# The first 60 microseconds of a fused retention and SiLU kernel: weight slice first, filler multiplies, transposes issued in parts

## The chip, the cores and the metric

The kernel runs on one core of a Trainium2 chip. Its engines are TensorE (PE in the profile; its weight loads are PEld), VectorE (DVE), ScalarE (ACT), GpSimd (POOL) and SyncE (SP), which only issues DMAs here. Each engine works through its own queue in order; they meet through semaphores. The metric is the device time of one execution in microseconds; lower is better.

## The reference

A recurrent retention layer is followed by a feed-forward block. q, k and v are 4 batches x 8 heads x 768 steps x 64 in float32; the two weights arrive as float64 (512 x 2048 and 2048 x 512).

```python
for t in range(S):
    state = gamma[None, :, None, None] * state + np.einsum('bhd,bhe->bhde', k[:, :, t], v[:, :, t])
    y[:, :, t] = scale * np.einsum('bhd,bhde->bhe', q[:, :, t], state)
...
x = np.ascontiguousarray(attn_out.transpose(0, 2, 1, 3)).reshape(B * S, H * D)
h = x @ w_in
g = h * (1.0 / (1.0 + np.exp(-h)))
return (g @ w_out).astype(np.float32)
```

## The kernel before

**Units.** The sequence is cut into 6 chunks of 128 steps. A unit is one chunk of one batch with all 8 heads; units are numbered chunk by chunk, so units 0 to 3 are chunk 0 of the four batches. For each unit the kernel

- loads k, q and v, 256 KB each, by one DMA each on SP's queue (`load`, L158);
- `T(n)` (`stage_t`): turns k and q, four 128x128 transposes each on TensorE (kp, qp), which ScalarE copies to SBUF (kt, qt);
- `K(n)` and `Q(n)`: scale k in place and the turned q by powers of gamma on VectorE; `KA(n)` does the former by eight instructions on ScalarE;
- `SC(n)`: 32 products of k with v (`stage_s`, the sums for the state; they read the scaled k) and 32 products of k with q (`stage_a`, the scores; they read kt and the scaled qt);
- `A(n)`, called three times (`steps_a`): the scores times a decay mask (am, L470), then the state in the middle of the chunk (mid), then the state behind it;
- `YA(n)` and `YB(n)` (`stage_y`): am with v, then q with the states, in two parts; between the parts stands a fence, a memset on POOL that waits for the first part and releases the second;
- `X(n)`, called four times (`steps_y`, `split_x`): copy y from PSUM (ys, L542), and split it into three float32r parts, xh on ScalarE (L557), xl (L560) and the third (L563) on VectorE.

**Products with w_in.** w_in is worked through in 16 column slices of 128. A slice is loaded by three DMAs (512 KB in all, `load_w`, two staging buffers) and converted from float64 words and split into three float32r parts in eleven steps, one for each `W(i)` (`early_slice`): the first, the eighth and the tenth are on ScalarE (L196, L120, L126), the other eight on VectorE (L199, L202, L206, L209, L212, L217, L123, L128). `P(n)` multiplies one slice with the four units of one chunk: twelve products of 128x128 by 128x512, eight into ha and four into hb. `CL(n)`, three times, closes it: a copy on ScalarE, a subtraction on VectorE, SiLU on ScalarE; `put_g` sends the result to DRAM. When all 96 results are made, they are read back, split and multiplied with w_out, which is prepared in the same way.

**The order.** TensorE's instructions are issued in program order throughout. For the first part of the kernel, up to `early_order.close()`, those of the other four queues are too: the calls `T(0), K(0)` and so on, one line after another, are the order of every queue. Behind that point the order of VectorE, ScalarE and SP is left to the planner of the framework, with a few instructions tied behind others. Up to that point the order holds units 0 to 7, the slices 0, 1 and 2 and the products P(0), P(1), P(2) with chunk 0 and P(16), which is the first one with chunk 1.

**PSUM.** kp, ha and hb share three banks in turn (`turn`); qp has a bank of its own, the scores and sums have two, y has two.

**The places that the change touches.** The loads at the top put k, q and v of units 0 to 5 on SP's queue in order, with slice 0 behind unit 0 and slice 1 behind unit 3. The identity that the transposes multiply with is made by POOL at 1.0 to 1.3 us. `next_chunk` rescales the powers of gamma for the next chunk by four instructions on ScalarE. `nc.scalar.activation(out=token, ...)` has no use but to load the table of SiLU early.

Of the kernel before, what the change touches and what calls it, by code (L numbers as in the profile page):

```python
# [13 lines left out]
FP32 = mybir.dt.float32  # L14
# [19 lines left out]
def kernel(  # L34
# [131 lines left out]
    def load_w(i):  # L166
        if i >= 2 * NF:
            return
        if wide:
            t = stage.tile([128, 2 * DM], U32, tag="wf", name=f"wf_{i}")  # L170
            w_in, w_out, n = moe_w_in.bitcast(U32), moe_w_out.bitcast(U32), 256
        else:
            t = stage.tile([128, DM], FP32, tag="wf", name=f"wf_{i}")
            w_in, w_out, n = moe_w_in, moe_w_out, 128
        if i < NF:
            to = t.rearrange("p (i o f) -> o p i f", o=2, f=n)
            src = w_in[:, ts(i, n)].rearrange("(i o p) f -> o p i f", o=2, p=128)
            nc.sync.dma_start(out=to[0], in_=src[0])
            for j in range(2):
                nc.sync.dma_start(out=to[1, ts(j, D)], in_=src[1, ts(1 - j, D)])  # L180
        else:
            nc.sync.dma_start(out=t, in_=w_out[ts(i - NF, 128), :])
        staged[i] = t
# [103 lines left out]
    def begin_w():  # L287
# [10 lines left out]
    early_order.enter_context(tc.manual_schedule(engines={  # L298
        mybir.EngineType.SP, mybir.EngineType.DVE, mybir.EngineType.Activation,
        mybir.EngineType.Pool}))  # L300
    for n in range(EARLY - 2):
        for name in "kqv":
            load(name, n)
        if n in (0, 3):
            load_w(n // 3)


    ident = const.tile([128, 128], FP32, tag="ident", name="ident")
# [54 lines left out]
    def banks(tag, name, n=2):  # L363
        return ps_u.tile([128, n, 512], FP32, tag=tag, name=name)
# [3 lines left out]
    def turn(name):  # L368
        turns[0] += 1
        return ps_h.tile([128, 512], FP32, tag=f"h{turns[0] % 3}", name=name)  # L370
# [55 lines left out]
        nc.scalar.copy(out=to[n].bitcast(U16).rearrange("p a (t w) -> p w a t", w=2),  # L426
                       in_=turned.pop((name, n)).rearrange("p (w a) t -> p w a t", w=2))

    def stage_t(n):

        for name, to, bufs, src, tp in (
                ("kt", kt, 2, kqv["k"][n], turn(f"kp_{n}")),
                ("qt", qt, 3, kqv["q"].pop(n), banks("q", f"qp_{n}", 1)[:, 0])):
            tp = tp.rearrange("p (a t) -> p a t", a=HP)
            for a in range(HP):
                nc.tensor.transpose(tp[:, a, :], src[:, 2 * a : 2 * a + 2, :], ident)  # L436
            to[n] = one.tile([128, HP, C], FP32, tag=name, name=f"{name}_{n}", bufs=bufs)
            evac[:] = [nc.scalar.copy(out=to[n], in_=tp).ins]

    def score_tile(n):  # L440
        u = banks("s", f"sc_{n}")
# [90 lines left out]
    def steps_y(n, yp):  # L532
        c, b = units[n]
        if b == 0:
            p, tag = (wpool, "wq") if c == LATE else (xpool, "xt")
            xt[c] = p.tile([128, 3, KIN, NT], FP32R, tag=tag, name=f"xt_{c}")
        raw = None
        if c < LATE:
            if n == 0:
                raws.append(wpool.tile([128, LATE * B, KIN, C], FP32, tag="wq", name="ys"))  # L540
            raw = raws[0][:, n]
            nc.scalar.copy(out=raw.rearrange("p a (o t) -> p o a t", o=2), in_=yp)  # L542
        elif c == LATE:
            raw = hpool.tile([128, KIN, C], FP32, tag="hs", name=f"ys_{n}")
            nc.scalar.copy(out=raw.rearrange("p a (o t) -> p o a t", o=2), in_=yp)
            nc.sync.dma_start(out=y_dram[b], in_=raw)
        yield from split_x(c, b, yp, raw)
# [179 lines left out]

    sa, ys, asteps, ysteps = {}, {}, {}, {}

    def T(n):  # L730
        stage_t(n)

    def SC(n):
        sa[n] = sc, sums = score_tile(n)
        stage_s(n, sums)
        stage_a(n, sc)
        asteps[n] = steps_a(n, sc, sums)

    def A(n):
        next(asteps[n], None)  # L740
# [10 lines left out]
    def X(n):  # L751
        next(ysteps[n], None)
# [12 lines left out]

    K, Q = scale_k, scale_q

    T(0), K(0)
    nc.scalar.activation(out=token, in_=lgc[:1, :1], func=AF.Silu)
    SC(0), A(0), Q(0), A(0), A(0)  # L770
    W(0), W(0), W(0), W(0), W(0)
    YA(0), YB(0), X(0)
    T(1), K(1)
    W(0)
    load_w(2)
    W(0)
    X(0), X(0)
    SC(1), A(1)
    W(0)
    A(1)  # L780
    Q(1), A(1)
    T(2), K(2)
    W(0), X(0)
    W(0), W(0)
    YA(1), SC(2)
    A(2)
    YB(1), X(1)
    A(2), Q(2), A(2)
    X(1)
    T(3), K(3)  # L790
    X(1), X(1)
    YA(2), YB(2), X(2)
    SC(3), A(3), A(3), Q(3), A(3)
    X(2), W(1), W(1)
    X(2), X(2)
    YA(3), YB(3), X(3), X(3)
    W(1), W(1)
    T(4)
    X(3), X(3)
    K(4)  # L800
    W(1), W(1)
    loads(EARLY - 2), loads(EARLY - 1)
    closing = {}

# [7 lines left out]
    def KA(n):  # L812
        t = kqv["k"][n]
        for h in range(H):
            nc.scalar.activation(out=t[:, h, :], in_=t[:, h, :], func=AF.Copy,
                                 scale=gk[:, units[n][0], h : h + 1])

    P(0)
    next_chunk()
    SC(4)  # L820
    CL(0), CL(0), CL(0)
    put_g(0)
    W(1)
    T(5)
    A(4), A(4), Q(4), K(5), A(4)
    W(1), W(1)
    YA(4), SC(5), YB(4)
    loads(EARLY)
    load_w(3)
    W(2), W(1)  # L830
    A(5)
    W(1), W(2), W(2)
    X(4)
    T(6)
    P(1)
    A(5), Q(5), A(5)
    KA(6)
    W(2), W(2), W(2)
    load("k", EARLY + 1), load("q", EARLY + 1)
    load_w(4)  # L840
    W(2)
    CL(1), CL(1)
# [184 lines left out]
```

## Time and profile before

| | us |
|---|---|
| median of 5 runs | 621.65 |
| lowest and highest | 621.46, 623.22 |
| the profiled execution | 621.65 |
| its span | 619.9 |
| TensorE busy | 604.3 (97%) |
| VectorE busy | 422.8 (68%) |
| ScalarE busy | 312.8 (50%) |
| first transpose of unit 0 | 4.18 |
| first product P(0) starts | 28.20 |

The profile is of one execution. Its times count from the start of the span; the execution took 1.75 us more than the span. In a timeline row stand the start, the duration, the engine, the line of the program, the operation, what is written and read, shapes, and how many such instructions follow each other; in brackets the idle time of the engine before it and what ended that. The slices of the page cut the span into 40 equal parts of 15.5 us; a digit is the busy share in tenths. In rows of groups of instructions three durations (least, median, most, in ns) are followed by the start of the first and of the last one.

### The profile page before, as it was taken

How to read it: one execution, taken by the hardware profiler on the slowest of the kernel's cores; microseconds unless marked ns; L12 is line 12 of the kernel's file. 1: busy time of each engine (PE TensorE's matmuls, PEld its weight loads, DVE VectorE, ACT ScalarE, POOL GpSimd, SP SyncE). 2: the span in 40 equal slices, each digit the busy share in tenths (PEclk: the TensorE clock that was granted, in tenths of full speed). 3: DMA queues.
4: the chain of work that ended last, by engine and by line, in shares of the span. 5: the costliest groups of instructions: out<-in, count | busy, mean ns of one | idle time of the engine just before them, and what ended most of it. 6: DMA issues, size and time to landing. Idle time of an engine off the chain costs nothing.

```text
span 619.9 us, 13494 instructions
## 1 busy us (share of the span) xinstructions
PE 604.3 (97%) x5384; PEld 498.0 (80%) x5384; DVE 422.8 (68%) x731; ACT 312.8 (50%) x595; POOL 22.0 (4%) x79
## 2 busy tenths in 40 slices
PE   6898999999999999999999999999999999999997
PEld 5777887888888888788788888888888888888886
DVE  4999889889789876767599783644635454554631
ACT  6678896676654666765587741312221221412311
POOL 3000000000001111110000000000000000000000
PEclk9999999999999999999999999999999999999999
DMA  9999896564667999989767542432523433442301
GB/s 193 218 216 217 221 250 195 167 191 166 221 162 220 247 252 212 264 230 277 271 224 262 194 154 68 156 116 83 186 72 120 153 102 102 138 134 85 120 1 68
DMA packets 137998, 107.31 MB, mean 173 GB/s; under 512 B 94800, under 2 KB 103248, under 8 KB 137936
## 3 DMA queue, kind: packets, MB, share of 16 engines
q1 hardware_dynamic: 135056, 101.21, 57.6%
q10 hardware_dynamic: 2880, 5.24, 2.3%
q8 instruction: 42, 0.69, 0.5%
q14 instruction: 20, 0.16, 0.1%
HBM read 66.06 MB, written 36.70 MB: 166 GB/s over the span
## 4 chain that ended last, share of the span: by engine, by line
PE 82%; ACT 1%; DMA 1%; SPq 0%; issue 0%; DVE 0%; DVEq 0%; POOLq 0%
PE ha L650 24%; PE o L967 21%; PE oa L967 14%; PE hb L650 12%; PE ob L967 7%; PE y L501 2%; PE sc L462 1%; PE sc L452 1%; DMA qw<-qp 1%; PE o L975 0%; SPq L676 0%; PE oa L975 0%; ACT qt L426 0%; PE qp L436 0%; PE kp L436 0%; ACT kt L426 0%
## 5 line engine op out<-in xcount | busy, mean ns | idle before, releaser
L650 PE MATMUL ha<-xt,wi 128*128 128x512 f32 x768 | 193.6, 394 | 1.1 <-ACT xt L557 0.7
L650 PEld LDWEIGHTS ha<-xt,wi 128*128 128x128 f32 x768 | 141.9, 188 | 33.2 <-ACT wi L126 1.2
L967 PE MATMUL o<-wo,gs 128*128 128x512 f32 x564 | 143.2, 389 | 0.0
L717 DVE TENSOR_TENSOR gs<-gr,gs 128x512 fp32r<-128x512 f32 x96 | 62.1, 685 | 90.3 <-ACT gs L715 90.3
L967 PEld LDWEIGHTS o<-wo,gs 128*128 128x128 f32 x564 | 105.9, 188 | 21.9
L715 ACT ACTIVATE gs<-gr 128x512 fp32r<-128x512 f32 x96 | 53.6, 621 | 134.2 <-issue 131.8
L967 PE MATMUL oa<-wo,gs 128*128 128x512 f32 x376 | 115.8, 389 | 0.0
L650 PE MATMUL hb<-xt,wi 128*128 128x512 f32 x384 | 103.1, 390 | 0.8 <-DVE g L665 0.7
L665 DVE TENSOR_TENSOR g<-g,hb 128x512 f32<-128x512 f32 x96 | 65.6, 683 | 44.5 <-ACT g L660 25.9
L650 PEld LDWEIGHTS hb<-xt,wi 128*128 128x128 f32 x384 | 71.8, 188 | 16.9 <-DVE g L665 1.1
L670 ACT ACTIVATE g<-g 128x512 f32<-128x512 f32 x96 | 60.3, 628 | 46.3 <-DVE g L665 46.2
L967 PEld LDWEIGHTS oa<-wo,gs 128*128 128x128 f32 x376 | 70.6, 188 | 14.7
L967 PE MATMUL ob<-wo,gs 128*128 128x512 f32 x188 | 73.7, 392 | 0.0
L660 ACT ACTIVATE g<-ha 128x512 f32<-128x512 f32 x96 | 57.0, 594 | 31.6 <-PE ha L650 13.2
L718 DVE SCALAR_TENSOR_TENSOR gs<-gs 128x512 fp32r<-128x512 f32 x96 | 62.0, 683 | 0.0
L967 PEld LDWEIGHTS ob<-wo,gs 128*128 128x128 f32 x188 | 35.3, 188 | 8.7 <-DVE o L985 1.6
L196 ACT ACTIVATE ca<-wf 128x512 f32<-128x512 f32 x32 | 21.3, 667 | 7.4 <-DVE cw L217 6.2
L212 DVE SCALAR_TENSOR_TENSOR ca<-wf,ca 128x512 f32<-128x512 uint32 x32 | 22.7, 709 | 0.5
L984 ACT ACTIVATE o<-o 128x512 f32<-128x512 f32 x10 | 6.0, 600 | 33.4 <-PE o L967 33.0
L206 DVE SCALAR_TENSOR_TENSOR cs<-ca,cs 128x512 uint32<-128x512 uint32 x32 | 22.1, 690 | 0.9
L501 PE MATMUL y<-qt,mid 64*64 64x64 f32 x384 | 20.3, 224 | 1.5 <-POOL token L377 1.5
L470 DVE TENSOR_TENSOR am<-sc,decay 128x512 f32<-128x512 f32 x24 | 16.5, 686 | 6.1 <-PE sc L462 6.0
(93 smaller groups left out, 562.0 us busy)
## 6 DMA issues: line engine op xcount, KB each, us to landing
gd<-g SPq DMA_DIRECT2D x96, 256.0 KB, 3.2
gr<-gd SPq DMA_DIRECT2D x96, 256.0 KB, 2.7
wf<-in_moe_w_out_dram SPq DMA_DIRECT2D x16, 512.0 KB, 4.4
out_dram<-o ACTq DMA_DIRECT2D x20, 256.0 KB, 2.1
wf<-in_moe_w_in_dram SPq DMA_DIRECT2D x16, 256.0 KB, 4.2
wf<-in_moe_w_in_dram SPq DMA_DIRECT2D x32, 128.0 KB, 4.2
kf<-in_k_dram SPq DMA_DIRECT2D x16, 256.0 KB, 5.2
qf<-in_q_dram SPq DMA_DIRECT2D x16, 256.0 KB, 4.4
```

The source lines that it names most:

```text
L196: nc.scalar.activation(out=a.bitcast(FP32), in_=hi.bitcast(FP32), func=AF.Abs, scale=65536.0)
L206: nc.vector.scalar_tensor_tensor(out=s, in0=a, scalar=3, in1=s, op0=ALU.logical_shift_left, op1=ALU.bitwise_or)
L212: nc.vector.scalar_tensor_tensor(out=p.bitcast(FP32), in0=lo, scalar=2.0 ** -52, in1=p.bitcast(FP32), op0=ALU.mult, op1=ALU.mult)
L501: i = nc.tensor.matmul(yp[ts(e, D), o, a, :], lhsT=lhsT, rhs=rhs, start=(e, o) not in started, stop=True, skip_group_check=True).ins
L650: nc.tensor.matmul(hb if i == 2 else ha, lhsT=w_sb[f][:, i, ts(kk, 128)], rhs=xt[c][:, i, kk, :], start=kk == 0 and i != 1, stop=kk == KIN ...
L660: copied[:] = [nc.scalar.activation(out=hs, in_=ha, func=AF.Copy, scale=ONE_E).ins]
L665: taken_out[:] = [nc.vector.tensor_tensor(out=hs, in0=hs, in1=hb, op=ALU.subtract).ins]
L670: nc.scalar.activation(out=hs, in_=hs, func=AF.Silu)
L715: nc.scalar.activation(out=t[:, 0, :], in_=g, func=AF.Copy, scale=HALF)
L717: nc.vector.tensor_tensor(out=t[:, 1, :], in0=g, in1=high, op=ALU.subtract)
L718: nc.vector.scalar_tensor_tensor(out=t[:, 2, :], in0=t[:, 1, :].bitcast(FP32), scalar=-1.0 / EPS, in1=high, op0=ALU.mult, op1=ALU.add)
L967: nc.tensor.matmul(o, lhsT=g, rhs=wo[f][:, i, :], start=f == 0 and i != 1, stop=f == NF - 1 and i != 0)
```

## The change

Seven things are changed, all in the ordered part:

- slice 0 of w_in is loaded ahead of k, q and v of unit 0; slice 1 stays behind unit 3;
- `keep_busy` is new: it multiplies the identity with itself n times into a bank that nobody reads. 17 such multiplies stand ahead of everything on TensorE, 3 ahead of Y(1), 3 and 2 around the first part of Y(3);
- five conversion steps of slice 0 come ahead of T(0), and the table of SiLU is loaded ahead of T(0) too;
- `stage_t` can turn k and q separately, and the transposes of k and of q stand apart: of unit 1 ahead of YA(0) and behind it, of unit 2 behind YA(1) and behind YB(1), of unit 3 ahead of YA(2) and behind it, of unit 4 ahead of P(0) and behind it;
- for units 0 to 3 the copy ys is left out: xh and xl read y from PSUM. Units 4 to 7 keep the copy;
- `next_chunk` is written ahead of P(0);
- between P(0) and P(1) the steps of slices 1 and 2 are ordered anew, P(1) comes ahead of T(6), and the loads of k and q of unit 9 come ahead of slice 3.

```diff
--- before.py
+++ after.py
@@ -298,11 +298,12 @@
     early_order.enter_context(tc.manual_schedule(engines={
         mybir.EngineType.SP, mybir.EngineType.DVE, mybir.EngineType.Activation,
         mybir.EngineType.Pool}))
+    load_w(0)
     for n in range(EARLY - 2):
         for name in "kqv":
             load(name, n)
-        if n in (0, 3):
-            load_w(n // 3)
+        if n == 3:
+            load_w(1)
 
 
     ident = const.tile([128, 128], FP32, tag="ident", name="ident")
@@ -426,16 +427,24 @@
         nc.scalar.copy(out=to[n].bitcast(U16).rearrange("p a (t w) -> p w a t", w=2),
                        in_=turned.pop((name, n)).rearrange("p (w a) t -> p w a t", w=2))
 
-    def stage_t(n):
-
-        for name, to, bufs, src, tp in (
-                ("kt", kt, 2, kqv["k"][n], turn(f"kp_{n}")),
-                ("qt", qt, 3, kqv["q"].pop(n), banks("q", f"qp_{n}", 1)[:, 0])):
+    def stage_t(n, names="kq"):
+
+        for name in names:
+            if name == "k":
+                to, bufs, src, tp = kt, 2, kqv["k"][n], turn(f"kp_{n}")
+            else:
+                to, bufs, src, tp = qt, 3, kqv["q"].pop(n), banks("q", f"qp_{n}", 1)[:, 0]
             tp = tp.rearrange("p (a t) -> p a t", a=HP)
             for a in range(HP):
                 nc.tensor.transpose(tp[:, a, :], src[:, 2 * a : 2 * a + 2, :], ident)
-            to[n] = one.tile([128, HP, C], FP32, tag=name, name=f"{name}_{n}", bufs=bufs)
+            to[n] = one.tile([128, HP, C], FP32, tag=f"{name}t", name=f"{name}t_{n}", bufs=bufs)
             evac[:] = [nc.scalar.copy(out=to[n], in_=tp).ins]
+
+    def keep_busy(n, t=None):
+        t = turn(f"none_{turns[0]}") if t is None else t
+        for _ in range(n):
+            nc.tensor.matmul(t[:, :128], lhsT=ident, rhs=ident, start=True, stop=True)
+        return t
 
     def score_tile(n):
         u = banks("s", f"sc_{n}")
@@ -535,8 +544,8 @@
             p, tag = (wpool, "wq") if c == LATE else (xpool, "xt")
             xt[c] = p.tile([128, 3, KIN, NT], FP32R, tag=tag, name=f"xt_{c}")
         raw = None
-        if c < LATE:
-            if n == 0:
+        if B <= n < LATE * B:
+            if n == B:
                 raws.append(wpool.tile([128, LATE * B, KIN, C], FP32, tag="wq", name="ys"))
             raw = raws[0][:, n]
             nc.scalar.copy(out=raw.rearrange("p a (o t) -> p o a t", o=2), in_=yp)
@@ -727,8 +736,8 @@
 
     sa, ys, asteps, ysteps = {}, {}, {}, {}
 
-    def T(n):
-        stage_t(n)
+    def T(n, names="kq"):
+        stage_t(n, names)
 
     def SC(n):
         sa[n] = sc, sums = score_tile(n)
@@ -765,40 +774,27 @@
 
     K, Q = scale_k, scale_q
 
+    keep_busy(17)
+    W(0, 5)
+    nc.scalar.activation(out=token, in_=lgc[:1, :1], func=AF.Silu)
     T(0), K(0)
-    nc.scalar.activation(out=token, in_=lgc[:1, :1], func=AF.Silu)
-    SC(0), A(0), Q(0), A(0), A(0)
-    W(0), W(0), W(0), W(0), W(0)
-    YA(0), YB(0), X(0)
-    T(1), K(1)
-    W(0)
+    W(0, 3)
     load_w(2)
-    W(0)
+    SC(0), A(0), W(0), A(0), Q(0), A(0)
+    T(1, "k"), K(1), W(0)
+    YA(0), T(1, "q"), YB(0), W(0)
     X(0), X(0)
-    SC(1), A(1)
-    W(0)
-    A(1)
-    Q(1), A(1)
-    T(2), K(2)
-    W(0), X(0)
-    W(0), W(0)
-    YA(1), SC(2)
-    A(2)
-    YB(1), X(1)
-    A(2), Q(2), A(2)
-    X(1)
-    T(3), K(3)
-    X(1), X(1)
-    YA(2), YB(2), X(2)
-    SC(3), A(3), A(3), Q(3), A(3)
-    X(2), W(1), W(1)
-    X(2), X(2)
-    YA(3), YB(3), X(3), X(3)
-    W(1), W(1)
-    T(4)
-    X(3), X(3)
-    K(4)
-    W(1), W(1)
+    SC(1), X(0), A(1), A(1), Q(1), X(0), A(1)
+    keep_busy(3)
+    YA(1), T(2, "k"), K(2), YB(1), X(1), X(1)
+    T(2, "q"), X(1), X(1)
+    SC(2), A(2), T(3, "k"), A(2), Q(2), K(3), A(2)
+    YA(2), T(3, "q"), YB(2), X(2), X(2)
+    SC(3), X(2), A(3), A(3), Q(3), A(3), X(2)
+    none = keep_busy(3)
+    YA(3), keep_busy(2, none), YB(3), X(3), X(3), W(1), W(1), X(3), X(3)
+    T(4, "k"), K(4)
+    W(1, 3)
     loads(EARLY - 2), loads(EARLY - 1)
     closing = {}
 
@@ -815,28 +811,31 @@
             nc.scalar.activation(out=t[:, h, :], in_=t[:, h, :], func=AF.Copy,
                                  scale=gk[:, units[n][0], h : h + 1])
 
+    next_chunk()
     P(0)
-    next_chunk()
+    CL(0), T(4, "q")
     SC(4)
-    CL(0), CL(0), CL(0)
+    CL(0), CL(0)
     put_g(0)
-    W(1)
+    W(1, 3)
+    A(4)
     T(5)
-    A(4), A(4), Q(4), K(5), A(4)
+    A(4), Q(4), K(5), A(4)
     W(1), W(1)
     YA(4), SC(5), YB(4)
+    W(1)
     loads(EARLY)
+    load("k", EARLY + 1), load("q", EARLY + 1)
     load_w(3)
-    W(2), W(1)
+    W(2)
     A(5)
-    W(1), W(2), W(2)
+    W(2), W(2)
     X(4)
+    P(1)
     T(6)
-    P(1)
     A(5), Q(5), A(5)
     KA(6)
     W(2), W(2), W(2)
-    load("k", EARLY + 1), load("q", EARLY + 1)
     load_w(4)
     W(2)
     CL(1), CL(1)
```

## The prediction

> **What bounds the kernel now.** I read the page's busy shares and slices first, then the waits, the timelines of TensorE and VectorE up to 64 us, and the landing times of the loads.
>
> ```profile
> PE 604.3 (97%) x5384; PEld 498.0 (80%) x5384; DVE 422.8 (68%) x731; ACT 312.8 (50%) x595; POOL 22.0 (4%) x79
> ...
> PE   6898999999999999999999999999999999999997
> ...
> DVE  4999889889789876767599783644635454554631
> ```
>
> TensorE is full from about 64 us to the end (its visible waits after that add up to little more than a microsecond, most of it one of 0.7 at 98), so only the start can be shortened, and a delay that is still there at 64 us reaches the end. In the first four slices VectorE is about as full as TensorE. Its timeline gives the pace: the mask product (am) of each of the first four units.
>
> ```profile
> 5.37 0.69 DVE L398 TENSOR_TENSOR kqv<-kqv,gk 128x512 f32<-128x512 f32 x1 [5.37 <-PE kp L436]
> 8.54 0.69 DVE L470 TENSOR_TENSOR am<-sc,decay 128x512 f32<-128x512 f32 x1 [2.48 <-PE sc L462]
> ...
> 15.70 0.69 DVE L470 TENSOR_TENSOR am<-sc,decay 128x512 f32<-128x512 f32 x1
> ...
> 19.58 0.68 DVE L470 TENSOR_TENSOR am<-sc,decay 128x512 f32<-128x512 f32 x1
> ...
> 23.70 0.69 DVE L470 TENSOR_TENSOR am<-sc,decay 128x512 f32<-128x512 f32 x1 [0.65 <-PE sc L462]
> ```
>
> VectorE idles 5.4 us before its first instruction and 2.5 before the second; from 12.9 to 23.0 it has no gap. Units 1, 2 and 3 follow one another in 3.9 and 4.1 us. The first product, P(0), starts at 28.20. TensorE runs slowly at first:
>
> ```profile
> L436 PE MATMUL kp<-ident,kqv x8: 421/421/472, 4.2 to 12.4; 128*128 128x128 f32 x8
> ...
> L436 PE MATMUL kp<-ident,kqv x4: 272/272/332, 26.8 to 27.2; 128*128 128x128 f32 x4
> ```
>
> The same transposes take 421 ns until 12 us and 272 ns at 27; from issue to issue it is 0.22 and 0.11 us. The switch lies near 17.5, where unit 1's score part of y is short already (0.75 us against 1.14 at 9.3). A third stretch matters, 36 to 42 us:
>
> ```profile
> 36.54 0.66 PE L436 MATMUL kp<-ident,kqv 128*128 128x128 f32 x4
> ...
> 37.39 2.09 PE L650 MATMUL ha<-xt,wi 128*128 128x512 f32 x8
> ...
> 38.25 2.02 ACT L815 ACTIVATE kqv<-kqv,gk 128x64 f32<-128x64 f32 x8
> ...
> 39.32 1.08 PE L650 MATMUL hb<-xt,wi 128*128 128x512 f32 x4
> ...
> 40.18 0.58 ACT L660 ACTIVATE g<-ha 128x512 f32<-128x512 f32 x1
> ...
> 41.08 0.65 PE L452 MATMUL sc<-kqv 64*64 64x64 f32 x32
> ```
>
> T(6) precedes P(1), so ScalarE's eight scalings KA(6), which overwrite what T(6) reads, run under P(1)'s 2.7 us, and SC(6), which needs them, waits for nothing.
>
> **The change, part by part.**
>
> *Slice 0 first.* Three DMAs (512 KB) move ahead of k, q and v of unit 0 on SP's queue. In before k0, q0, v0 land at 4.05, 5.27, 6.38 (issue plus time to landing), 1.15 us per 256 KB, and the slice at 8.7. So now: slice about 5.6, k0 6.4, q0 7.6, v0 8.6. k1 (9.7) and all behind it keep their place, since the bytes ahead of them are the same. T(0) is 2.3 us later. In exchange VectorE does four conversion steps (0.42, 0.42, 0.69, 0.43) in its old gap, then K(0) and two more (0.69 each), to about 9.9. The Silu table load (1.28 us) now stands ahead of T(0)'s copies; it ends at 7.8, before q's transposes do: nothing; uncovered, 0.7.
>
> *Filler.* 17 multiplies from about 1.3 us, when the identity is made. The nearest row, transposes of the same shape, gives 0.22 us each: 3.8 us, over at 5.1, before k0 lands: free. The Trainium skill ("FP8 and Floating Point Precision", TensorE Precision Notes) has true FP32 make four passes; by that, 17 take some 7.3 us on the slow clock and push T(0) back by up to 2. The trace speaks against it: 32 score products of 64 columns issue in 0.46 us, 58 ns in each of four quadrants, about half of what four passes over 64 columns would take at the rate of the 512-column products (0.227 us each). I take 3.8. The later fillers (8 multiplies, 0.9 us on the full clock) stand where TensorE waits for a mask or a fence anyway: nothing, at most 0.9.
>
> *What the clock buys.* The rows first: slow from 4.18 to 17.5 although TensorE worked most of that time, with gaps of 0.8 us at 8.5 and 0.3 at 10.9. The skill ("TensorE: Matmul & The Clock Gate", Part 1: The HAM clock gate) lets one busy window of about 3.4 us lift the throttle. By the rule the clock is full at 5 to 8 us and P(0) falls where the sum below puts it. By the row a gapless window is wanted, which comes after k0, at 11 to 14: T, SC and Y of unit 0 then take about 0.45 us more each, and I let 0.6 of it reach P(0), the rest lying beside conversion steps. I take the middle, 0.3.
>
> *Transposes parted; the loop.* From mask 1 to mask 2 there is now: mask 0.69, hop 0.12, score part of Y 0.53, its first state part 0.40 to the result (T(2,k) beside it), fence through POOL 0.28, then Y's other half with the transposes of q behind it. Counted from that half's start, q's transposes are ready at 0.9, ScalarE is through with xh at 1.0, copies qt in 0.59, hop 0.1, second half of SC 0.65, hop 0.07: 2.4. Sum 4.4, with xl and the third part of x ahead of the mask 4.5. The same walk gives 4.6 from mask 0 to 1 (L123 waits for L120, Q(0) for L123, Y for Q(0)) and 4.1 from 2 to 3 (q turned ahead of the fence, but xh and xl between its copy and the mask). In before T(n+1) is issued ahead of Y(n), so the copies are made while VectorE masks; hence 3.9 to 4.1, partly on the slow clock. The first mask follows L217, at 10.0. So masks at 10.0, 14.6, 19.1, 23.2; with the clock's 0.3 the last is at 23.5 (before: 23.70).
>
> *x from PSUM.* The copy ys goes (0.59 us, four times, ScalarE). Reading PSUM costs the same in later chunks (xt<-y 682 ns on VectorE against 685 from SBUF; 583 against 631 on ScalarE). The y banks are now held until xl is made, but Y(n+1) waits for a mask issued behind xl or just ahead of it: nothing, at most 0.6 a unit. On the path is the last copy: P(0) follows the last mask by 0.69+0.12+0.53+0.40+0.28+0.40+0.63+0.05 = 3.1, where it was 4.5 (the copy 0.6; a wait of 0.7 at 25.75 behind the fence, with no work to explain it; small hops). I let 0.8 of such waits come back. P(0): 23.5+3.1+0.8 = 27.4, a gain of 0.8.
>
> *Around P(0).* On ScalarE next_chunk stays ahead of CL(0): nothing. T(4,q) goes behind P(0), and the second half of SC(4) waits for its copy: 0.8 us of TensorE, beside which VectorE has L212 and L217; half, 0.4, stays. Slice 1 is two steps behind at P(0) and made up: L128 near 36.9, needed by P(1)'s last third at 37.9. Gain left when P(1) is due: 0.4.
>
> *P(1) ahead of T(6).* With that 0.4: Y(4) ends at 36.0, P(1) runs 36.1 to 38.8, T(6) ends at 39.95, its copies at 40.6, KA(6) 40.5 to 42.5, SC(6) starts at 42.6 (was 41.08). CL(1) is queued behind KA(6) on ScalarE: g at 42.5 (was 40.18), so VectorE's subtraction at 43.2 (was 42.10), L123 behind it at 43.8, the next mask at 44.6 (was 43.50). T(7) and P(2) follow SC(6): P(2) at 44.7 (was 43.21). Against before that is 1.5 late on TensorE and 1.1 on VectorE, whose gaps until 57 come to under 0.6. I carry 1.3: the swap takes 1.7. Were SC(6) let in head by head as KA(6) goes on, it would take 1.2.
>
> *Loads.* k9 and q9 (two DMAs, 1.5 us of SP's queue) go ahead of load_w(3), which lands at 48 instead of 46.6; its first use is at 57.5, so 9 us cover it; without that cover it costs 1.5. POOL's fences keep their order and only move with Y.
>
> Sum: 0.4 gained, 1.7 lost, +1.3 us. Against the profiled execution, 619.9 of span plus 1.75 around it = 621.65, which is also the median of the five: 623.0.
>
> **The rivals.**
>
> *It evens out* (0.22). None of those waits returns and the clock is full at 6: P(0) at 26.3, 1.9 early, 1.5 left when P(1) is due; the swap takes 1.7: 621.9. For it: the 0.7 at 25.75 has no visible cause. Against: almost the same instruction stream feeds TensorE.
>
> *TensorE's clock set the pace* (0.20, faster). If a unit takes 3.5 us on the full clock instead of 4.4, the last mask comes 2.7 us sooner, P(0) at 24.7, and +1.3 becomes −1.4: 620.2. For it: TensorE's rows halve. Against: VectorE had no gap from 12.9 to 23.0, has 3.3 us of work per unit, and the period did not shrink at 17.5 (3.9, then 4.1). It decides from 4.0 us per unit (even) and 3.6 (faster).
>
> *The filler doesn't do what it says* (0.12, slower). Clock slow to 17.5, or four passes: P(0) 1.1 to 2 later than summed: 624 to 625.
>
> **How the numbers follow.** About 0.2%, 1.24 us, is what a measurement of this kernel can tell from no change. The likeliest is the lost cover of KA(6), 0.46, with 622.3 to 624.2 as its own range; with the filler's 0.12 slower has 0.58, same 0.22, faster 0.20. The sum lies close to the line between same and slower, but the swap's 1.2 to 1.7 is the surest term in it. The range reaches from the fast clock's case to the slow filler's: 620.0 to 625.2.
>
> **What would show it.** Right: kp<-ident at 272 ns before 14 us; masks some 4.4 us apart; P(0) between 27 and 28; SC(6) behind KA(6), with TensorE idle 1.7 us before it; P(2) near 44.7; the same gaps from 64 us on. Wrong: masks less than 4.0 us apart and P(0) before 26; SC(6) not waiting; gaps that close between 57 and 100 us.

## The result, and the profile after

The changed kernel takes 623.83 us, the median of 43 runs (622.11 to 628.31); the kernel before, run beside it, takes 622.07 us, the median of 80 runs (618.96 to 625.62). The ratio is 1.0032, with a 95% interval from 1.0023 to 1.0041: 2.0 us slower, 1.4 to 2.6. The forecast was 623.0. The profiled execution took 623.9 us, its span 622.1.

The page of the changed kernel, busy shares and slices:

```profile
PE 609.6 (98%) x5434; PEld 503.2 (81%) x5434; DVE 421.8 (68%) x731; ACT 311.3 (50%) x591; POOL 23.1 (4%) x79
...
PE   8989999999999999999999999999999999999997
...
DVE  5779899898888976857599793644636454554631
```

TensorE's first slice rises from 6 to 8 tenths, as the filler now counts as work; the third falls from 9 to 8. The 5.3 us more of busy time are not work on the result: the filler's own rows add up to 8.4 us. (Line 479 of the changed kernel is the mask of line 470 before; 659, 669 and 674 are the lines 650, 660 and 665, which make ha and hb, the copy g and the subtraction; 446 is the filler; 399 was 398, 439 was 436, 461 and 471 were 452 and 462, 510 was 501, 566 and 569 were 557 and 560, 811 was 815.)

VectorE's timeline: the first conversion step, K(0), and the masks of units 0 to 3.

```profile
5.53 0.43 DVE L199 TENSOR_SCALAR cs<-wf 128x512 uint32<-128x512 uint32 x1 [5.53 <-DMA wf<-in_moe_w_in_dram]
...
7.76 0.69 DVE L399 TENSOR_TENSOR kqv<-kqv,gk 128x512 f32<-128x512 f32 x1
...
10.23 0.69 DVE L479 TENSOR_TENSOR am<-sc,decay 128x512 f32<-128x512 f32 x1 [0.45 <-PE sc L471]
...
14.79 0.68 DVE L479 TENSOR_TENSOR am<-sc,decay 128x512 f32<-128x512 f32 x1
...
19.59 0.68 DVE L479 TENSOR_TENSOR am<-sc,decay 128x512 f32<-128x512 f32 x1
...
23.83 0.68 DVE L479 TENSOR_TENSOR am<-sc,decay 128x512 f32<-128x512 f32 x1
```

The first mask is 1.7 us later than before, the last one only 0.13. All of this is made up between the first two masks (4.56 us apart, 7.16 before), where conversion steps of slice 0 stood. The two distances behind that are longer than before: 4.80 and 4.24 us, against 3.88 and 4.12. P(0) starts at 27.21 (28.20 before). It follows the last mask by 3.38 us instead of 4.50: some 0.65 of the difference is the copy of y that is gone, some 0.5 the wait at 25.75 in the profile before, which this execution doesn't have.

Of this gain nothing is left at the mask of unit 4, here before and after:

```profile
32.57 0.69 DVE L470 TENSOR_TENSOR am<-sc,decay 128x512 f32<-128x512 f32 x1
```

```profile
32.58 0.68 DVE L479 TENSOR_TENSOR am<-sc,decay 128x512 f32<-128x512 f32 x1
```

VectorE works from 27.19 to this mask without a gap, and two conversion steps of slice 1 (L202 and L206), which came ahead of P(0) before, now lie in this stretch. From the start of P(0) to the mask of unit 4 it takes 5.37 us, 4.37 before; in the eight kernels below that put these steps in the same place and have no slow stretch there, it takes 5.36 or 5.37. Y(4) waits for the mask and starts at 33.31 on TensorE in both kernels.

The rows of the filler and of the first transposes (least, median and most ns, then the first and last start):

```profile
L446 PE MATMUL none<-ident x34: 274/300/582, 1.4 to 6.9; 128*128 128x128 f32 x34
...
L439 PE MATMUL kp<-ident,kqv x4: 272/272/273, 7.0 to 7.3; 128*128 128x128 f32 x4
```

The transposes of unit 0 run at 272 ns at once, where they took 421 before. So the filler did what it says. Its 17 multiplies are recorded as 34.

Now the stretch from P(1) to P(2), on TensorE, ScalarE and VectorE:

```profile
37.19 0.28 PE L471 MATMUL sc<-qt,kt 64*64 64x64 f32 x3 [0.85 <-issue]
...
37.69 2.12 PE L659 MATMUL ha<-xt,wi 128*128 128x512 f32 x8
39.64 1.08 PE L659 MATMUL hb<-xt,wi 128*128 128x512 f32 x4
40.55 0.60 PE L439 MATMUL kp<-ident,kqv 128*128 128x128 f32 x4
...
42.21 2.02 ACT L811 ACTIVATE kqv<-kqv,gk 128x64 f32<-128x64 f32 x8
...
42.62 1.94 PE L461 MATMUL sc<-kqv 64*64 64x64 f32 x29 [0.17 <-ACT kqv L811]
...
44.13 0.58 ACT L669 ACTIVATE g<-ha 128x512 f32<-128x512 f32 x1
...
44.74 0.69 DVE L674 TENSOR_TENSOR g<-g,hb 128x512 f32<-128x512 f32 x1 [2.02 <-ACT g L669]
...
46.10 2.09 PE L659 MATMUL ha<-xt,wi 128*128 128x512 f32 x8
```

Two things are to be seen. SC(6) starts at 42.62 and its state part takes 1.94 us instead of 0.65: the products are let in head by head as KA(6) goes through its eight scalings, so most of the wait hides in the length of the row, and only 0.17 us stand in its bracket. And behind KA(6) on ScalarE stands g, at 44.13 (40.18 before), for which VectorE waits 2.02 us. P(2) starts at 46.10, 2.9 us later than before.

How late the changed kernel is against before, read in the two profiles at the start of each product's hb: 1.0 early at P(0), 0.3 late at P(1), 2.7 at P(2), 3.1 at P(3), 2.4 from 108 us on, 3.1 at 193 us, 2.2 from 281 us to the end.

### The profile page after: what moved, and what is told of

It is laid out like the page before. It is cut to its first block, busy times and chain, and to the rows that moved or that the text cites. A ratio compares the mean times of both kernels' runs of the same rounds, so it can differ in the third digit from the quotient of the medians.

```text
span 622.1 us, 13595 instructions
## 1 busy us (share of the span) xinstructions
PE 609.6 (98%) x5434; PEld 503.2 (81%) x5434; DVE 421.8 (68%) x731; ACT 311.3 (50%) x591; POOL 23.1 (4%) x79
## 4 chain that ended last, share of the span: by engine, by line
PE 81%; DMA 1%; ACT 0%; SPq 0%; issue 0%; DVE 0%; DVEq 0%; POOLq 0%
PE ha L659 24%; PE o L966 21%; PE oa L966 14%; PE hb L659 12%; PE ob L966 7%; PE y L510 2%; PE sc L471 1%; DMA kw<-kp 1%; PE sc L461 1%; PE o L974 0%; PE oa L974 0%; ACT kt L427 0%; SPq L420 0%; PE qp L439 0%; PE kp L439 0%
## 5 line engine op out<-in xcount | busy, mean ns | idle before, releaser
L669 ACT ACTIVATE g<-ha 128x512 f32<-128x512 f32 x96 | 57.0, 594 | 27.4 <-PE ha L659 10.3
L206 DVE SCALAR_TENSOR_TENSOR cs<-ca,cs 128x512 uint32<-128x512 uint32 x32 | 22.1, 691 | 0.9
L984 DVE TENSOR_TENSOR o<-o,o 128x512 f32<-128x512 f32 x10 | 6.8, 688 | 19.3 <-ACT o L983 19.3
```

The source lines that it names most:

```text
L206: nc.vector.scalar_tensor_tensor(out=s, in0=a, scalar=3, in1=s, op0=ALU.logical_shift_left, op1=ALU.bitwise_or)
L669: copied[:] = [nc.scalar.activation(out=hs, in_=ha, func=AF.Copy, scale=ONE_E).ins]
```

## The experiments

Each ratio is to the kernel before, run on the same chip, with its 95% interval. About seven in ten executions of the kernel before lie within 1.5 us of its median, the outermost 3.1 below and 3.6 above, so the ratios judge the times, and the profiles, each of one execution, only the steps. A ratio is not the quotient of two medians (1.0028 for the change).

### What the swap costs

**T(6) ahead of P(1) again, all else as changed** (a_noswap).

```diff
-    P(1)
     T(6)
+    P(1)
     A(5), Q(5), A(5)
```

> The changed kernel with T(6) back ahead of P(1), nothing else. Theory S (the lost cover of KA(6) is the main loss): SC(6) waits for nothing, P(2) starts 1.5 to 2.5 us earlier than in the changed kernel (46.10), at about 44, and the time falls by 1.5 to 2 us, to the level of the kernel before or under it. Rival L (the loss is in the first four units or in the reordered conversion steps): P(2) moves by under 0.5 and the time stays within 0.5 us of the changed kernel. The unexplained TensorE gap near 36.2 should stay, since nothing ahead of it is changed.

Measured: 622.6 us, ratio 1.0010 (0.9991 to 1.0029). The time does what theory S says; the profiled execution does not show it. Its P(2) starts at 46.78, not near 44: a TensorE gap of 1.40 us (shown in the last section) stands ahead of T(6), and behind the gap TensorE runs slowly until about 41 us, so that T(6)'s transposes of k take 1.11 us instead of 0.66. The run c_best below has the same order without the gap.

**The swap alone, in the kernel before** (b_swap).

```diff
-    T(6)
     P(1)
+    T(6)
     A(5), Q(5), A(5)
```

> The kernel before with P(1) ahead of T(6), nothing else. Theory S: P(0) unchanged at 28.2, P(1) some 0.8 us earlier (36.5), KA(6) behind P(1), SC(6) at about 43 instead of 41.1, P(2) near 45 instead of 43.2, and the time 1.3 to 2 us longer than before. Rival L: under 0.5 us longer.

Measured: 623.93 us, ratio 1.0033 (1.0019 to 1.0048). The steps are those of the changed kernel:

```profile
42.24 2.02 ACT L815 ACTIVATE kqv<-kqv,gk 128x64 f32<-128x64 f32 x8
...
42.65 1.94 PE L452 MATMUL sc<-kqv 64*64 64x64 f32 x29 [0.17 <-ACT kqv L815]
...
46.13 1.17 PE L650 MATMUL ha<-xt,wi 128*128 128x512 f32 x4
```

That the times agree with the changed kernel's to 0.03 us is chance: in this execution P(0)'s products ran slowly for a while (its hb begins 3.02 us behind its ha, 1.98 before), so P(1) starts at 37.73 and not near 36.5. The distances are what counts.

The swap alone costs as much as the whole change; without it the change cannot be told from no change. What it costs can be read apart from all that comes earlier, from the start of the pair P(1) and T(6), whichever is first, to the start of P(2):

| kernel | first of the pair | starts | P(2) | between |
|---|---|---|---|---|
| before | T(6) | 36.54 | 43.21 | 6.67 |
| c_best (below) | T(6) | 36.60 | 43.33 | 6.73 |
| changed | P(1) | 37.69 | 46.10 | 8.41 |
| b_swap | P(1) | 37.73 | 46.13 | 8.40 |
| a_nofill (below) | P(1) | 38.08 | 46.48 | 8.40 |
| a_fill13 (below) | P(1) | 36.24 | 44.65 | 8.41 |

P(2) in the kernel before, for the first line of the table:

```profile
43.21 2.29 PE L650 MATMUL ha<-xt,wi 128*128 128x512 f32 x8
```

The pair is the same work in both orders, and the swap adds 1.7 us. Four more kernels with T(6) first take 6.64 to 6.91 (b_psum, c_copy, a_pipe, b_fill), and a_noswap 7.65, with T(6) on the slow clock.

**Which of the two waits carries it?** Three kernels take one away each. First, K(6) in place of KA(6): one VectorE instruction scales k of unit 6, and ScalarE is free (a_k6).

```diff
-    KA(6)
+    K(6)
```

> The changed kernel with P(1) still ahead of T(6), but unit 6's k scaled by one VectorE instruction (0.69 us) in place of KA(6)'s eight on ScalarE. If KA(6) without cover is what P(1) ahead of T(6) costs, SC(6) starts right behind Y(5), the copy of ha(1) leaves ScalarE's queue 2 us earlier, and P(2) starts at 44 to 44.8 instead of 46.1; VectorE has 0.69 more to do; the time falls by about 1 to 1.5 us. If the order of P(1) and T(6) costs in another way (slice 2's steps, PSUM banks), P(2) stays within 0.5 of 46.1.

Measured: 623.64 us, ratio 1.0034 (1.0020 to 1.0049); the stretch takes 7.48.

```profile
41.22 0.69 DVE L399 TENSOR_TENSOR kqv<-kqv,gk 128x512 f32<-128x512 f32 x1 [0.98 <-PE kp L439]
...
42.29 0.65 PE L461 MATMUL sc<-kqv 64*64 64x64 f32 x32
...
43.50 0.62 PE L471 MATMUL sc<-qt,kt 64*64 64x64 f32 x26 [0.45 <-issue]
...
46.53 1.20 PE L659 MATMUL ha<-xt,wi 128*128 128x512 f32 x4 [0.17 <-ACT wi L126]
```

SC(6) waits no more and takes 0.65 us again. But VectorE stands 0.98 us before K(6), since T(6) is late, and works 0.69 on it; the steps of slice 2 behind it are late by that, and P(2) is stopped half way by the second part of slice 2. One wait is gone, another has come in its place: at the start of P(2) 0.9 us of 1.7 are won in this execution, at its hb, behind that stop, 0.5 (9.86 us from the start of P(1), 10.34 in the changed kernel). The ratio (1.0034, against 1.0032) doesn't show them.

Second, the first closing step of P(1) ahead of KA(6) on ScalarE (c_g1).

```diff
     A(5), Q(5), A(5)
+    CL(1)
     KA(6)
...
-    CL(1), CL(1)
+    CL(1)
```

> The changed kernel with the first closing step of P(1), the copy g on ScalarE, ahead of KA(6) instead of behind it. If the time is lost because VectorE's subtraction, the steps of slice 2 and the next mask queue behind that copy, P(2) comes 1 us or more earlier than 46.1 although SC(6) starts up to 0.6 later, and the ratio falls to about 1.002. If it is lost because SC(6) waits for KA(6), P(2) is 0 to 0.6 later and the ratio stays at 1.003 to 1.004.

Measured: 624.36 us, ratio 1.0036 (1.0021 to 1.0051).

```profile
37.08 2.11 PE L659 MATMUL ha<-xt,wi 128*128 128x512 f32 x8
...
41.59 0.61 ACT L669 ACTIVATE g<-ha 128x512 f32<-128x512 f32 x1
42.08 2.01 ACT L811 ACTIVATE kqv<-kqv,gk 128x64 f32<-128x64 f32 x8
...
42.24 0.69 DVE L674 TENSOR_TENSOR g<-g,hb 128x512 f32<-128x512 f32 x1
...
42.50 1.93 PE L461 MATMUL sc<-kqv 64*64 64x64 f32 x29 [0.66 <-ACT kqv L811]
...
45.97 2.08 PE L659 MATMUL ha<-xt,wi 128*128 128x512 f32 x8
```

g comes 2.5 us earlier and VectorE's subtraction with it, but P(2) at 45.97, hardly sooner than 46.10. As P(1) started 0.6 us earlier in this execution, the stretch even grew, from 8.41 to 8.89: KA(6) now stands behind g. So the queue behind KA(6) is not what sets P(2); SC(6) waiting for KA(6) is, the second of the two cases expected. The other runs say the same: in all six kernels with P(1) first and KA(6) in the program (the changed one, b_swap, a_nofill, a_fill13, c_half, c_g1) P(2) starts 1.87 us after the last scaling of KA(6) ends. In the seven with T(6) first it starts 2.9 to 3.2 us after it. With a_k6 the picture is: SC(6) comes last, and the steps of slice 2 come next, less than a microsecond behind.

Third, only q's transposes behind P(1) (c_half). KA(6) needs k turned, not q.

```diff
+    T(6, "k")
     P(1)
-    T(6)
+    T(6, "q")
```

> The changed kernel with the transposes of k of unit 6 ahead of P(1) and those of q behind it. KA(6) needs the former alone. If the cover of KA(6) is what the swap took away, SC(6) waits for nothing, P(2) comes at 43.5 to 44.5 (46.1 in the changed kernel) and the ratio to the kernel before falls to 1.000 to 1.002. If it is the late copies of q (or ScalarE's queue as a whole, with SiLU of P(1) behind it) that cost, P(2) stays at 45 to 46 and the ratio at 1.002 to 1.004.

Measured: 623.72 us, ratio 1.0016 (1.0003 to 1.0030); the stretch takes 8.27.

```profile
41.50 0.59 ACT L441 COPY qt<-qp 128x512 f32<-128x512 f32 x1 [2.56 <-PE qp L439]
41.98 2.02 ACT L811 ACTIVATE kqv<-kqv,gk 128x64 f32<-128x64 f32 x8
```

This kernel does not try what it was made for: on ScalarE the copy of q's transposes still stands ahead of KA(6), waits 2.56 us for P(1) and the transposes behind it, and holds KA(6) where it was. TensorE's order was mended and ScalarE's was not. The interval overlaps that of the changed kernel, so the lower ratio says nothing.

### What the filler and the clock are worth

**No filler at all** (a_nofill): the 25 multiplies are left out of the changed kernel.

```diff
-    keep_busy(17)
...
-    keep_busy(3)
...
-    none = keep_busy(3)
-    YA(3), keep_busy(2, none), YB(3), X(3), X(3), W(1), W(1), X(3), X(3)
+    YA(3), YB(3), X(3), X(3), W(1), W(1), X(3), X(3)
```

> The changed kernel without any filler multiply. Clock theory: the clock comes up only at 11 to 15 us, the first transposes take 421 ns again, the masks of units 0 to 3 come 0.3 to 1 us later, P(0) at 27.6 to 28.2. Theory F (the TensorE gap of 1.1 us at 36.2 without a releaser sits at a fixed place in the count of TensorE's instructions, and the filler's 50 recorded multiplies and their 50 loads moved it onto a burst of 64-column products): without the filler it goes from 36.2, and P(1) comes no later than in the changed kernel although P(0) does; the time is then within 0.5 us of the changed kernel's. Rival (the gap belongs to that moment, or to what is loaded then): the gap stays at 36 and the time is 0.5 to 1 us longer.

Measured: 624.61 us, ratio 1.0030 (1.0014 to 1.0047); the kernel before took 621.57 beside it, and the quotient of these medians would be 1.0049, so the third decimal is uncertain. The full clock, read from the issue times of equal multiplies, comes at about 13 us (5.0 in the changed kernel). The masks stand at 11.50, 16.07, 20.87 and 25.12: each about 1.3 us later, with the same distances to within 0.02 us. P(0) is 1.5 later, at 28.74. Not all of that is the clock: v of unit 0, for which SC(0) waits in both kernels, landed at 9.3 in this execution and at 8.9 in the changed kernel's, so that about 1.1 is left. The gap near 37 us is gone, as expected. Of the 1.5 us 0.4 are left at P(1) against the changed kernel, whose execution loses time to that gap; against a_fill13, which has none, P(0), P(1) and P(2) are each 1.8 later. In the time neither difference can be told.

**13 multiplies at the start and none later** (a_fill13).

```diff
-    keep_busy(17)
+    keep_busy(13)
...
-    keep_busy(3)
...
-    none = keep_busy(3)
-    YA(3), keep_busy(2, none), YB(3), X(3), X(3), W(1), W(1), X(3), X(3)
+    YA(3), YB(3), X(3), X(3), W(1), W(1), X(3), X(3)
```

> The changed kernel with 13 filler multiplies at the start instead of 17 and none later. 13 run from 1.37 to about 6.0 and still lift the clock at about 5, so masks and P(0) stay as in the changed kernel (P(0) 27.2 within 0.3). Theory F: a place in TensorE's stream at the old count lies 24 recorded multiplies further on, past Y(4) and at the start of P(1), whose products take 0.227 us each; so the gap in SC(5) goes or shrinks, P(1) starts near 36.8 instead of 37.69 and the time falls by 0.5 to 1 us. Rival: gap and time as in the changed kernel.

Measured: 623.59 us, ratio 1.0022 (1.0006 to 1.0039). P(0) starts at 26.90 and P(1) at 36.24, with no gap ahead of P(1). At 119 us this execution was only 0.6 late; between 193 and 246 us it lost 1.9 more, 1.4 of it at a TensorE gap without a visible cause near 200, the rest where TensorE waits for ScalarE's copy of a turned k near 240.

**The filler alone, in the kernel before** (b_fill); `keep_busy` itself is added as in the change.

```diff
+    keep_busy(6)
     T(0), K(0)
     nc.scalar.activation(out=token, in_=lgc[:1, :1], func=AF.Silu)
     SC(0), A(0), Q(0), A(0), A(0)
+    keep_busy(3)
```

> The kernel before with 6 filler multiplies ahead of T(0) and 3 between SC(0) and Y(0), nothing else. If VectorE sets the pace of the first units (my prediction), an earlier clock alone buys nothing: masks of units 2 and 3 and P(0) within 0.5 us of before (19.58, 23.70, 28.2), time within 1 us of before. Rival (TensorE's clock sets the pace): once the clock is up early, masks come closer than 3.6 us and P(0) before 26.5. Should the clock still come at 17 us, six multiplies are too few, and this tells nothing on the rival.

Measured: 623.35 us, ratio 1.0020 (1.0007 to 1.0034). The full clock comes at about 4.4 us.

```profile
7.92 0.69 DVE L476 TENSOR_TENSOR am<-sc,decay 128x512 f32<-128x512 f32 x1 [2.16 <-PE sc L468]
...
14.35 0.69 DVE L476 TENSOR_TENSOR am<-sc,decay 128x512 f32<-128x512 f32 x1 [0.49 <-PE sc L468]
...
18.23 0.68 DVE L476 TENSOR_TENSOR am<-sc,decay 128x512 f32<-128x512 f32 x1
...
22.84 0.69 DVE L476 TENSOR_TENSOR am<-sc,decay 128x512 f32<-128x512 f32 x1 [1.14 <-PE sc L468]
```

With the full clock through the whole loop, units 1 to 3 follow each other in 3.9 and 4.6 us (3.9 and 4.1 before): TensorE's clock does not set the pace. The first mask to the second, 6.4 us, became 0.7 shorter, and the third to the fourth 0.5 longer; TensorE waited 1.08 us there for q of unit 3 to land, so the loads are the next bound. This execution was the fastest of its 22 (619.28). Why their median lies above that of before stays open.

### What reading y from PSUM is worth

**In the old order alone** (b_psum).

```diff
-        if c < LATE:
-            if n == 0:
+        if B <= n < LATE * B:
+            if n == B:
```

> The kernel before with xh and xl of units 0 to 3 read from PSUM (no copy ys), nothing else. P(0) some 0.6 us earlier than in before when no unexplained TensorE gap lies ahead of it (27.0 to 27.6), the rest of the early part the same amount earlier or nothing of it left at P(2); time within 0.7 us of before.

Measured: 626.69 us, ratio 1.0072 (1.0057 to 1.0086), the slowest of all.

```profile
22.46 0.73 PE L501 MATMUL y<-am,kqv 64*64 64x64 f32 x32 [2.21 <-DVE xt L560]
...
29.08 1.13 PE L501 MATMUL y<-am,kqv 64*64 64x64 f32 x32 [2.77 <-DVE xt L560]
...
33.16 3.69 PE L650 MATMUL ha<-xt,wi 128*128 128x512 f32 x8
```

Y(2) and Y(3) wait 2.21 and 2.77 us for xl of the unit before, which holds the banks of y: in the old order xl stands behind the next mask in VectorE's queue. P(0) starts at 33.16, 5 us later than before instead of 0.6 earlier. The waits are not the whole price: behind the second one equal work takes longer (Y(3)'s row 1.13 us, 0.69 before; the eight products into ha 3.69 us, 2.14 before), the mark of the slow clock. No run parts the two.

**The copies put back in the new order**, with T(6) first (c_copy): the same lines the other way round.

```diff
-        if B <= n < LATE * B:
-            if n == B:
+        if c < LATE:
+            if n == 0:
```

> The changed kernel with T(6) ahead of P(1) and with the copy ys back for units 0 to 3. It prices x from PSUM in the new order. If leaving the copy out is worth the 0.6 us of ScalarE on the path from the last mask to P(0), P(0) comes 0.5 to 1 us later than with T(6) first alone (27.8 there), and the time is 0.5 to 1 us longer. If the copies in the loop matter too (0.6 us in each unit), the masks are 4.8 to 5.2 us apart and P(0) comes 2 to 3 us later. If holding the y banks had its price here as it had in the old order (5 us), this kernel is faster, by up to 1 us.

Measured: 625.80 us, ratio 1.0052 (1.0034 to 1.0069), against 1.0010 with T(6) first alone.

```profile
25.73 0.69 DVE L569 TENSOR_TENSOR xt<-ys,xt 128x512 fp32r<-128x512 f32 x1 [2.37 <-ACT xt L566]
26.34 0.68 DVE L479 TENSOR_TENSOR am<-sc,decay 128x512 f32<-128x512 f32 x1
...
30.46 2.11 PE L659 MATMUL ha<-xt,wi 128*128 128x512 f32 x8 [0.76 <-ACT xt L566]
```

The copy stands ahead of xh on ScalarE, xl waits for xh, and the next mask stands behind xl: the masks are 5.2, 5.8 and 4.9 us apart (4.6, 4.8 and 4.3 in a_noswap), and P(0) comes at 30.46 instead of 27.76. Leaving the copies out costs 4.5 us in one order, slow clock included, and earns 2.6 in the other.

### Two versions that were to beat both

**k and q turned ahead of Y in units 2 and 3, xl late** (a_pipe): the new start, with the transposes not parted.

```diff
-    keep_busy(17)
+    keep_busy(13)
...
-    SC(1), X(0), A(1), A(1), Q(1), X(0), A(1)
-    keep_busy(3)
-    YA(1), T(2, "k"), K(2), YB(1), X(1), X(1)
-    T(2, "q"), X(1), X(1)
-    SC(2), A(2), T(3, "k"), A(2), Q(2), K(3), A(2)
-    YA(2), T(3, "q"), YB(2), X(2), X(2)
-    SC(3), X(2), A(3), A(3), Q(3), A(3), X(2)
-    none = keep_busy(3)
-    YA(3), keep_busy(2, none), YB(3), X(3), X(3), W(1), W(1), X(3), X(3)
+    SC(1), X(0), A(1), A(1), T(2), Q(1), X(0), A(1), K(2)
+    YA(1), YB(1), X(1), X(1)
+    SC(2), A(2), A(2), X(1), T(3), Q(2), A(2), K(3), X(1)
+    YA(2), YB(2), X(2), X(2)
+    SC(3), A(3), A(3), X(2), Q(3), A(3), X(2)
+    YA(3), YB(3), X(3), X(3), W(1), W(1), X(3), X(3)
...
-    P(1)
     T(6)
+    P(1)
```

> A candidate from the changed kernel: T(6) ahead of P(1) again, the transposes of units 2 and 3 whole and ahead of Y of the unit before, so that ScalarE copies them while VectorE masks, 13 filler multiplies and none later. If the loop through Y, fence and transposes is what made the period 4.4, it goes to about 4.0 and P(0) comes at 25.5 to 26.7 instead of 27.2; P(2) near 42; the time 1 to 2 us under the kernel before, less what the stretch behind 100 us takes back. Rival (VectorE's own work or the loads set the period): masks stay 4.4 apart, P(0) near 27, time as with T(6) put back alone.

Measured: 625.57 us, ratio 1.0057 (1.0040 to 1.0073).

```profile
21.37 0.63 PE L439 MATMUL qp<-ident,kqv 128*128 128x128 f32 x4 [1.71 <-DMA kqv<-in_q_dram]
...
26.03 1.13 PE L510 MATMUL y<-am,kqv 64*64 64x64 f32 x32 [1.52 <-DVE xt L569]
```

It meets both walls: TensorE waits for q of unit 3, which has not landed, and Y(3) for the banks that xl holds. P(0) starts at 29.26, and TensorE is slow again behind the second wait (P(0)'s hb begins 3.56 us behind its ha, 1.98 before). Where neither wall stands, between the masks of units 1 and 2, whole transposes are the faster order: 4.26 us, against 4.80 in the changed kernel. So the parting doesn't make the loop faster by itself; with the late xl and the loads as they land here, the other order stops.

**T(6) first and 13 multiplies** (c_best).

```diff
-    keep_busy(17)
+    keep_busy(13)
...
-    keep_busy(3)
...
-    none = keep_busy(3)
-    YA(3), keep_busy(2, none), YB(3), X(3), X(3), W(1), W(1), X(3), X(3)
+    YA(3), YB(3), X(3), X(3), W(1), W(1), X(3), X(3)
...
-    P(1)
     T(6)
+    P(1)
```

> The changed kernel with T(6) ahead of P(1) again, 13 filler multiplies at the start instead of 17 and none later. If the swap was the one thing that cost time (0.3% = 2.0 us) and the fillers cost a few tenths, this stands at 0.998 to 1.001 of the kernel before, P(0) near 27, P(2) at 43 to 44. If it is the sum of the whole new order that costs, or if what is early at 60 us is taken back between 190 and 255 us by the waits for turned k, it stands at 1.001 to 1.003 and P(2) still comes before 44.

Measured: 622.57 us, ratio 1.0006 (0.9989 to 1.0023).

```profile
36.60 0.74 PE L439 MATMUL kp<-ident,kqv 128*128 128x128 f32 x4
...
37.53 2.09 PE L659 MATMUL ha<-xt,wi 128*128 128x512 f32 x8
38.39 2.03 ACT L809 ACTIVATE kqv<-kqv,gk 128x64 f32<-128x64 f32 x8
...
40.31 0.58 ACT L669 ACTIVATE g<-ha 128x512 f32<-128x512 f32 x1
...
41.21 0.65 PE L461 MATMUL sc<-kqv 64*64 64x64 f32 x32
...
43.33 2.09 PE L659 MATMUL ha<-xt,wi 128*128 128x512 f32 x8
```

KA(6) lies under P(1) again, SC(6) takes 0.65 us and waits for nothing. It was 0.6 us early at 119 us and 0.1 early at the end, in an execution (621.60 us) that was the fastest of its 14. No version here beats the kernel before by an amount that can be told.

## Why the prediction was right

**The sum** was 0.4 gained, 1.7 lost. The 1.7 holds: 8.41 against 6.67 us in the stretch, and the swap alone makes the kernel 0.33% slower. The 0.4 gained is not there: without the swap the kernel stands at +0.6 us, with an interval that holds nought. So the forecast, 1.35 us, fell short of the 2.0 by about the part that I booked as gain. The term for the swap carried the forecast; the paragraph on P(1) names the term that failed.

**Slice 0 first** went as worked out: VectorE starts on it at 5.53 (forecast 5.6). k of unit 0 landed at 6.5 (6.4).

**The filler's term was mis-sized.** I took 0.22 us for each multiply from the transposes, 3.8 us in all, against the four passes of the Trainium skill ("FP8 and Floating Point Precision", TensorE Precision Notes), which made 7.3. The row says that the skill was nearer: each multiply leaves two records, 0.213 us apart before the clock's switch at 5.0 and 0.11 behind it, so 0.43 and then 0.22 us, and the 17 ran from 1.37 to about 7.0. A transpose and a multiply of one shape are not one price. My evidence against the four passes was a miscount: a stage of scores is 16 products in the program, two records each, and not 32. 16 in 0.46 us are 115 ns for each in its quadrant, and four passes over 64 columns at 0.227 us for 512 make 113. The filler held T(0) up by half a microsecond; that cost nothing, as SC(0) waits for v of unit 0, which lands at 8.9. The 8 later multiplies, booked at nothing, cost about 0.3: P(0) follows the last mask by 3.37 or 3.38 us in the five kernels that have them and read y from PSUM at full clock, and by 3.09 in a_fill13 and c_best, which have none. That is the 3.1 of my sum, without the 0.8 that I let come back.

**The clock** came by the rule, not by the middle that I took: at 5.0 us, 3.7 after the filler began, as "TensorE: Matmul & The Clock Gate" (Part 1: The HAM clock gate) lets one busy window do. In the six kernels here with the 17 multiplies ahead it came between 4.7 and 7.1. What it is worth was mis-sized too: without any filler P(0) is 1.1 us later, the later load taken off, where I let 0.6 reach it.

**The loop**: masks forecast at 10.0, 14.6, 19.1 and 23.5 came at 10.23, 14.79, 19.59 and 23.83. The longest difference is 0.5 us. That the period would be longer than the 3.9 and 4.1 of before was forecast as well.

**x from PSUM** was right for the order it stands in (no wait for banks, P(0) at 27.21, forecast 27.4), and the bound of 0.6 a unit for held banks holds for that order alone: in the old one the waits are 2.21 and 2.77. The gain was mis-sized as well: I counted only the last copy, 0.6 us, and in the new order each of the four lies on the way to the next mask, 2.7 us at P(0).

**P(1)** is the step that failed: forecast 36.1, measured 37.69. Of slice 1 I wrote that it is two steps behind at P(0) and made up, and booked nothing for the making up. Those two steps, L202 and L206, take 1.0 us more of VectorE ahead of the mask of unit 4 (5.37 us from P(0), 4.37 before), and the gain at P(0), which I let shrink to 0.4, is gone there. That is 0.4 of the 1.6 us. Most of the rest is a TensorE gap inside SC(5) for which no engine is named: 0.85 us idle, 1.07 from issue to issue. Its size is that of one execution: in c_g1, the same program up to there, it is 0.52 from issue to issue and P(1) starts at 37.08. In a_fill13 the gap is gone and P(0) 0.3 sooner, and P(1) starts at 36.24, close to the forecast by chance.

**The swap**: SC(6) was forecast at 42.6 and P(2) at 44.7; SC(6) starts at 42.62, though P(1) was 1.6 late, because it is let in head by head, the variant that I had priced at 1.2; that the two figures agree is chance. The swap took the full 1.7, since the last head still waits for KA(6)'s end at 44.2. The queue behind KA(6) was named too, with g at 42.5 (44.13): true, but second, as c_g1 shows.

**The loads** of unit 9 ahead of slice 3 left no wait for slice 3, as forecast, though it landed near 51 instead of 48.

**The statement that a delay still there at 64 us reaches the end** holds in the main only. Of 3.1 us at 62 us, 2.4 were left at 108, since the kernel before waits longer for parts of a slice near 97 and 98 us than the changed one does near 101, and 2.2 at the end. (TensorE's idle time at 98 is 0.41 us, not the 0.7 that I read; 0.66 stand at 61.9.) Single executions shift by up to 2.6 us between 193 and 246 us (a_pipe).

**The rivals.** That TensorE's clock sets the pace fell with b_fill. That the filler does nothing fell with the 272 ns rows. That it evens out needed P(0) at 26.3 and 1.5 us of that lead still there at P(1); P(0) came at 27.21, and nothing was left.

## What to carry to other kernels

Before two instructions of one engine are exchanged, list what each of them releases: T(6) was short, but eight scalings, 2 us in all, were timed to lie under the product behind it. A step that is put off is not free because it fits in later: two conversion steps moved behind P(0) took the whole gain at P(0) back at the next mask. A wait can stand in the length of a row instead of its bracket (0.65 us became 1.94 with only 0.17 of idle time), so compare the durations of equal work, not the waits alone. Leaving a copy out frees an engine and holds its source longer; whether that earns or costs is a matter of where the reader stands in its queue, here 2.6 us won in one order and 4.5 lost in the other, part of it to the slow clock behind the waits.

## What the hardware showed that I had not expected

**Gaps without a releaser at fixed places in TensorE's stream.** Counted by the multiplies recorded ahead of it, and measured from issue to issue, a gap of 0.5 to 1.7 us sits at no. 1105 to 1107 in ten of the fourteen kernels, however the program is ordered, and one of 0.5 to 1.6 us at no. 727 or 728 in all six that issue 25 fillers, and in no other. 1106 and 728 are 378 apart. Others stand near no. 2628 or 2756. The rows show the idle part alone. Three of them, in this order: a_noswap at no. 728, the changed kernel at no. 1106, c_best at no. 2757.

```profile
38.28 0.38 PE L471 MATMUL sc<-qt,kt 64*64 64x64 f32 x3 [1.40 <-issue]
```

```profile
54.56 0.62 PE L461 MATMUL sc<-vf,kf 64*64 64x64 f32 x26 [0.65 <-issue]
```

```profile
199.75 0.21 PE L510 MATMUL y<-qt,mid 64*64 64x64 f32 x1 [1.30 <-issue]
```

The 728th multiply falls into the short 64-column products of SC(5) in the changed kernel. In a_fill13 it falls into P(1)'s 512-column products; in the kernel before it is a short product of Y(5), right behind P(1)'s twelve long ones; no gap is to be seen in either. In the two pairs that differ by 25 against 13 fillers alone (the changed kernel and a_fill13, a_noswap and c_best) the gap stands in the one with 25. So the filler, recorded as 50 multiplies, brought a pause to a place where it shows. That long products hide it elsewhere fits with this, but isn't shown, nor that the pauses are the fetching of instructions: the page's two instruction queues move 0.69 and 0.16 MB over the span, and one transfer of each falls into 34 to 36 us, ahead of the gap at 36 to 37.

**The slow rate comes back after long waits.** In five traces equal work on TensorE is slow again for some 2.5 to 7.5 us (products into ha issued 0.43 us apart instead of 0.227, transposes 0.21 instead of 0.11): a_noswap, b_swap, c_half, a_pipe and b_psum. In each a gap of 1.4 us or more came before it (1.40, 1.50, 1.50, 1.52, and 2.21 and 2.77). The other nine, whose longest gap behind 14 us is 1.30 (c_best), have none after the start. A gap of 1.71 in a_pipe was not followed by it at once, so the length of a gap alone doesn't decide. A wait on TensorE can so cost more than its own length.

**The clock row of the page** reads 9 in every slice of the kernels before and after alike. The slow clock shows only in the durations (421 against 272 ns) and the issue times of equal instructions.
